# Reordering the start of a fused state-space and GeGLU kernel: x tile 2 loaded second, gate products before up products, tile 0 centred from a plain sum

## The chip, the cores and the metric

One core of a Trainium2 chip. The metric is the device time of one execution in microseconds (us), taken as the median of several executions. A profiled execution has a time of its own and a span inside it: the span runs from the first to the last instruction that the profiler shows.

## The reference, cut to what matters

The input x has 2048 rows of 512 numbers in bf16. Each row is normalised, and two branches are computed from the result and added to x:

```python
xn = layernorm(x)                                   # (x - mean) / sqrt(var + 1e-5), per row
# branch A: a diagonal complex recurrence over the 2048 rows, 512 states
h[t] = Lam_bar * h[t-1] + B_bar @ xn[t]
yA = 2 * Re(h @ C.T) + xn * Dskip
# branch B: a GeGLU feed-forward with 1376 hidden columns
yB = (gelu(xn @ w_gate) * (xn @ w_up)) @ w_down
out = x + yA + yB
```

## The kernel before, in words

**Blocks and tiles.** The 2048 rows are four blocks of 512, and a block is four tiles of 128 rows. In the regular path a block is normalised on the vector engine (`LN`, L637), transposed by DMA on SP's queue (`TR`, L708), multiplied by the gate and up weights (`GU`, L801) and by B (`BU`, L715), rotated and scanned on the vector engine (`CHAIN`, L734), and summed into the output (`DN`, L837).

**The start is special.** For block 0 the kernel does not wait for a complete layer norm. It subtracts the mean from a tile (`sub`, L920), transposes the centred tile on TensorE and copies it out of PSUM on ScalarE (`cent_T`, L652, copy at L669), and multiplies it, centred but not scaled, with the weights (`GT_mm`, L675). The factor 1/sqrt(var) is applied when the products leave PSUM (`GT_evac`, L691: gelu on ScalarE at L696, the product with the up half on VectorE at L699). It does this for the first 896 hidden columns in four ranges (`FR`, two of 192 columns and two of 256). `unit(j, r)` is one tile j times one range r, with gate and up in one matmul per 128 rows of the weights. For tiles 0 and 1 and the ranges 0 and 1 the gate products (`[0]`) and the up products (`[1]`) are separate matmuls of 192 columns, so that the gate can start before the up weights are there. Products of one tile and range share a PSUM bank.

**Filling.** TensorE runs seven matmuls on constants first (`fwarm`, L899) and further ones on constants between the first pieces of work (`fill`, L905; their results are not used).

**Means.** Tile 0's mean comes from `stats` on VectorE (L611: bn_stats then bn_aggr), tile 1's from a ScalarE copy with an accumulator (L926). `root` (L616) adds epsilon, takes the square root on GpSimd (L620), and `recip` (L624) inverts on VectorE; tiles 0 and 1 share one such chain, tiles 2 and 3 another.

**What sets the order.** TensorE and SP run their work in the order in which the program text creates it. VectorE, ScalarE and GpSimd run in the order of a planner (`Sched`), which simulates all engines with written-down durations and chooses by latest start times; `order_behind` (L129), which `ch` (L917) uses, pins one operation behind another. A wait on a semaphore is put in where data cross engines or come by DMA.

**Loads at the start.** SP's queue issues tile 0 of x, the first half of the first gate chunk (`WG0h[0]`: weight rows 0 to 255, columns 0 to 383), tile 2, the first up chunk, tile 3, and then the next chunks. The second gate chunk waits for `WG0h[0]` on SP (L502, `after=[gate0]`). Behind these in SP's queue come `tr_par`, block 0's four transposes, the load of block 1, the two transposed loads of B, Dskip, the load of block 2, and block 1's transposes. ScalarE's queue issues tile 1, `WG0h[1]` and three small parameter rows.

Of the kernel before, what the change touches and what calls it, by code (L numbers as in the profile page):

```python
# [9 lines left out]
ALU = mybir.AluOpType  # L10
# [67 lines left out]
class Sched:  # L78
# [95 lines left out]
    def _backward(self, span):  # L174
        ops = self.ops
        left = {op.id: len(op.users) for op in ops}
        late = {op.id: span for op in ops}
        ready = {e: [] for e in ENGINES}
        last = {e: [op for op in ops if op.eng == e] for e in INORDER}
        for op in ops:  # L180
            if left[op.id] == 0 and op.eng not in INORDER:
                ready[op.eng].append(op)
        busy = {e: span for e in ENGINES}
        begin = {}
        n = len(ops)
        while n:
            best = None
            for e in ENGINES:
                if e in INORDER:
                    if not last[e] or left[last[e][-1].id]:  # L190
                        continue
                    op = last[e][-1]
                else:
                    if not ready[e]:
                        continue
                    op = max(ready[e], key=lambda o: (min(busy[e], late[o.id]), o.finish, o.id))
                end = late[op.id] if op.kind == "dma" else min(busy[e], late[op.id])
                if best is None or end > best[0]:
                    best = (end, op)
            end, op = best  # L200
            e = op.eng
            if e in INORDER:
                last[e].pop()
            else:
                ready[e].remove(op)
            begin[op.id] = end - op.dur
            if op.kind == "dma":
                begin[op.id] = min(begin[op.id], busy[e] - op.issue)
                busy[e] = begin[op.id]
            else:  # L210
                busy[e] = begin[op.id]
            n -= 1
            for d in op.deps:
                late[d.id] = min(late[d.id], begin[op.id] - LAT(d, op))
                left[d.id] -= 1
                if left[d.id] == 0 and d.eng not in INORDER:
                    ready[d.eng].append(d)
        return begin

    def _forward(self, prio):  # L220
# [11 lines left out]
        nleft = len(ops)  # L232

        def rdy_time(op):
            return max([d.finish + LAT(d, op) for d in op.deps] + [op.nb])

        while nleft:
            best = None
# [52 lines left out]
    def emit(self):  # L291
        nc, es = self.nc, self.es
        order = self.order
        esem = {}
        for e in ENGINES:
            if any(op.kind == "eng" for op in order[e]):
                esem[e] = es.enter_context(nc.semaphore("q_" + e))
        cnt = {e: 0 for e in ENGINES}
        nd = 0
        for e in ENGINES:  # L300
            for op in order[e]:
                if op.kind == "eng":
                    cnt[e] += 1
                    op.sem, op.val = esem[e], cnt[e]
                else:
                    op.sem, op.val = es.enter_context(nc.semaphore("d%d" % nd)), 16
                    nd += 1
        self.n_sems = len(esem) + nd
        plan = {}
        nwait = 0  # L310
        for e in ENGINES:
            seen = {}
            prog = []
            for op in order[e]:
                need = {}
                for d in op.deps:
                    if d.kind == "eng" and d.eng == e and (e == "tensor" or d is op.behind):
                        continue
                    key = ("e", d.eng) if d.kind == "eng" else ("d", d.id)
                    if seen.get(key, 0) >= d.val:  # L320
                        continue
                    if key not in need or need[key].val < d.val:
                        need[key] = d
                for key, d in need.items():
                    seen[key] = d.val
                waits = [(d.sem, d.val) for d in need.values()]
# [12 lines left out]
        for (s, v) in final_waits:  # L339
            nc.sync.wait_ge(s, v)  # L340
# [10 lines left out]
def d_pe(n_list):  # L351
    return sum(n / 2.4 + 2.5 for n in n_list)
# [4 lines left out]
D_TINY = 160.0  # L357
# [4 lines left out]
def build(nc, ins, out):  # L362
    with ExitStack() as es:
# [110 lines left out]
        NM1 = A.alloc("NM1", [1], F32)  # L474

        def ld_x(b):
            return S.dma(lambda e, b=b: e.dma_start(
# [26 lines left out]

        def load_par():
            for q, nm in enumerate(("A_log_dt", "A_Lambda_re", "A_Lambda_im")):
                S.dma(lambda e, q=q, nm=nm: e.dma_start(PROW.ap[4 * q:4 * q + 4, :], ins[nm].rearrange("(s p) -> s p", p=128)),
                      1024, writes=[PROWq[q]], tag="ld_" + nm, queue="scalar", after=[half])
# [128 lines left out]
        def LN(b, js=range(4)):  # L637
# [3 lines left out]
            recip(qb, rq)  # L641
            norms(b, js, mn, rq, js[0])

        def SKIP(b):
# [5 lines left out]
        XCd = lambda j, k: XC_all.ap[:, k, 128 * j:128 * (j + 1)]  # L650

        def cent_T(j, banks, engs="A"):  # L652
            per = KD // len(engs)
# [21 lines left out]
        def GT_mm(j, r, bank, us, ks=range(KD)):  # L675
# [1 line left out]
            w = f1 - f0  # L677
            ci = max(0, r - 1)
            Wc = [(WGc, WUc)[u][ci] for u in us]
            if ci == 0 and us == [0] and len(ks) == 2:  # L680
                Wc = [WG0h[ks[0] // 2]]
            dst = PS[bank][:, w * us[0]:w * (us[-1] + 1)].rearrange("p (w f) -> p w f", w=len(us))

            def f(e):
# [1 line left out]
                for k in ks:  # L686
                    ins_ = e.matmul(dst, XCd(j, k), WGU[:, us[0]:us[-1] + 1, k, f0:f1], start=(k == 0), stop=(k == KD - 1))  # L687
                return ins_
            PE(f, d_pe([w * len(us)] * len(ks)), Wc + XCs[j][ks[0] // 2:ks[-1] // 2 + 1], [BANK[bank]], "GT")

        def GT_evac(j, r, bank, rs):  # L691
            f0, f1 = FR[r]
# [227 lines left out]
        def sub(j):  # L920
# [2 lines left out]
        load_par()  # L923
        load_W()
        tr_par()
        ACT(lambda e: e.activation(H0[3].ap[:, 0:D], X[1].ap, ACTF.Copy, scale=-1.0 / D, accum_out=NM1.ap), d_act(512) + 90,  # L926
            [X[1]], [H0[3], NM1], "mean1")
        ch(*stats(0, 0)); ch(sub(0))
        ch(V(lambda e: e.tensor_scalar(XN[1].ap, X[1].ap, NM1.ap, None, ALU.add), d_dve_ts4x(512), [X[1], NM1], [XN[1]], "sub"))
# [36 lines left out]
        unit(0, 2)  # L966
        unit(1, 2)
        unit(3, 0); unit(3, 1)
# [95 lines left out]
```

## Time and profile before

| | |
|---|---|
| median of 9 runs | 177.88 us (177.43 to 178.19) |
| profiled execution, its own time | 177.99 us |
| its span | 176.2 us |
| TensorE matmul busy | 172.8 us, 98% of the span |
| VectorE busy | 162.4 us, 92% |
| ScalarE busy | 90.3 us, 51% |
| GpSimd busy | 9.8 us, 6% |

Busy time is the time in which an engine has an instruction under way. Matmuls overlap: one of 128x512 is shown with 379 ns, while 49 of them in a row take 10.74 us, so 0.219 us each. For TensorE, the distance from one start to the next is therefore what counts. "Landing" of a DMA is the moment when its last part has signalled.

### The profile page before, as it was taken

The numbers are of one execution on the slowest core, as the hardware profiler recorded it, in microseconds if no ns is written. First come the engines' busy times: TensorE is split into PE (matmuls) and PEld (weight loads), VectorE is DVE, ScalarE is ACT, GpSimd is POOL, SyncE is SP. The second block draws the span as 40 slices with busy tenths as digits, with TensorE's granted clock in tenths as the row PEclk, the third lists the DMA queues.
The fourth block names the chain that finished last, engine by engine and source line by source line (L and its number), as shares of the span: only waits on it lengthen the run. The fifth ranks groups of instructions, "written<-read, shape, count | busy, mean of one in ns | idle before, by whom it ended". The sixth has DMA issues, their size and how long they took to land.

```text
span 176.2 us, 2489 instructions
## 1 busy us (share of the span) xinstructions
PE 172.8 (98%) x876; PEld 85.2 (48%) x891; DVE 162.4 (92%) x283; ACT 90.3 (51%) x169; POOL 9.8 (6%) x25
## 2 busy tenths in 40 slices
PE   8999999999999999999999999999999999999995
PEld 3954464444644444444644444444464444444454
DVE  6979999986999999979999999989999999999981
ACT  5466558899876899002676793000667790000000
POOL 3212030210000000011000000000000000000000
PEclk9999999999999999999999999999999999999999
DMA  5997995974999000012015000002101000000141
GB/s 159 333 298 173 203 237 110 115 149 97 194 299 214 4 0 0 2 39 80 4 33 113 5 0 0 4 0 76 43 0 30 4 0 0 0 0 0 33 149 61
DMA packets 33396, 14.36 MB, mean 81 GB/s; under 512 B 23688, under 2 KB 33384, under 8 KB 33384
## 3 DMA queue, kind: packets, MB, share of 16 engines
q1 hardware_dynamic: 32944, 13.87, 34.2%
q10 hardware_dynamic: 440, 0.33, 0.7%
q8 instruction: 7, 0.11, 0.3%
q14 instruction: 5, 0.04, 0.1%
HBM read 6.46 MB, written 2.10 MB: 49 GB/s over the span
## 4 chain that ended last, share of the span: by engine, by line
PE 98%; issue 0%; DVE 0%
PE PS L853 37%; PE PS L812 32%; PE PS L723 16%; PE PS L687 7%; PE PS L786 3%; PE PS L902 2%; PE PS L662 1%; PE PS L909 0%; DVE arena L871 0%
## 5 line engine op out<-in xcount | busy, mean ns | idle before, releaser
L853 PE MATMUL PS<-arena 128*128 128x512 bf16 (+3 forms) x317 | 65.9, 366 | 0.3
L812 PE MATMUL PS<-arena 128*128 128x512 bf16 x258 | 57.5, 379 | 0.3
L853 PEld LDWEIGHTS PS<-arena 128*128 128x128 bf16 (+1 forms) x323 | 30.8, 98 | 35.2
L812 PEld LDWEIGHTS PS<-arena 128*128 128x128 bf16 x264 | 25.8, 98 | 30.5
L756 DVE TENSOR_TENSOR_SCAN arena<-arena 128x512 bf16<-128x512 f32 x32 | 38.8, 1253 | 0.0
L827 ACT ACTIVATE arena<-PS 128x512 bf16<-128x512 f32 x33 | 19.7, 598 | 36.9 <-PE PS L812 33.3
L723 PE MATMUL PS<-arena 128*128 128x512 bf16 x125 | 27.8, 379 | 0.2
L831 ACT ACTIVATE arena<-PS 128x512 bf16<-128x512 f32 x33 | 19.7, 597 | 4.8 <-PE PS L812 4.6
L845 ACT ACTIVATE PS<-arena 128x512 f32<-128x512 bf16 (+2 forms) x17 | 9.6, 581 | 20.4 <-PE PS L853 19.7
L723 PEld LDWEIGHTS PS<-arena 128*128 128x128 bf16 x128 | 12.5, 98 | 14.8
L727 ACT ACTIVATE arena<-PS 128x512 bf16<-128x512 f32 x32 | 17.6, 595 | 2.3 <-PE PS L723 2.3
L871 DVE TENSOR_TENSOR arena<-PS,arena 128x512 bf16<-128x512 f32 (+2 forms) x17 | 10.8, 652 | 5.0 <-PE PS L853 4.5
L833 DVE TENSOR_TENSOR arena<-arena 128x512 bf16<-128x512 bf16 x33 | 13.0, 416 | 1.7 <-ACT arena L831 1.6
L687 PE MATMUL PS<-arena 128*128 128x192 bf16 (+2 forms) x80 | 13.4, 325 | 0.0
L613 DVE BATCH_NORM_STATS2 arena<-arena 128x6 f32<-128x512 bf16 x16 | 10.3, 682 | 0.7 <-DMA arena<-in_A_x_dram 0.7
L687 PEld LDWEIGHTS PS<-arena 128*128 128x128 bf16 x80 | 7.6, 102 | 4.8 <-issue 0.2
L743 DVE TENSOR_TENSOR arena<-arena 128x4096 bf16<-128x4096 bf16 (+1 forms) x5 | 9.2, 1858 | 0.5 <-ACT arena L608 0.5
L745 DVE TENSOR_TENSOR arena<-arena 128x4096 bf16<-128x4096 bf16 (+1 forms) x5 | 9.2, 1859 | 0.4 <-ACT arena L609 0.4
L696 ACT ACTIVATE arena<-PS,arena 128x192 bf16<-128x192 f32 (+1 forms) x16 | 6.7, 447 | 5.0 <-PE PS L687 4.0
L768 DVE TENSOR_TENSOR arena<-arena 128x4096 bf16<-128x4096 bf16 x4 | 9.2, 2289 | 0.1
L769 DVE TENSOR_TENSOR arena<-arena 128x4096 bf16<-128x4096 bf16 x4 | 9.1, 2285 | 0.0
L699 DVE SCALAR_TENSOR_TENSOR arena<-PS,arena 128x192 bf16<-128x192 f32 (+1 forms) x16 | 6.6, 444 | 1.2 <-ACT arena L696 1.0
(84 smaller groups left out, 110.4 us busy)
## 6 DMA issues: line engine op xcount, KB each, us to landing
out_dram<-arena SPq DMA_DIRECT2D x15, 128.0 KB, 1.7
arena<-in_A_x_dram SPq DMA_DIRECT2D x3, 512.0 KB, 4.9
arena<-in_B_w_down_dram SPq DMA_DIRECT2D x1, 1280.0 KB, 8.2
arena<-in_B_w_gate_dram SPq DMA_DIRECT2D x2, 256.0 KB, 4.2
arena<-in_B_w_up_dram SPq DMA_DIRECT2D x2, 256.0 KB, 4.6
arena<-in_B_w_gate_dram SPq DMA_DIRECT2D x1, 480.0 KB, 5.8
arena<-in_B_w_up_dram SPq DMA_DIRECT2D x1, 480.0 KB, 6.2
arena<-arena SPq DMA_TRANSPOSE x25, 2.5
```

Source lines behind the costliest of these rows:

```text
L613: return (V(lambda e: e.bn_stats(ST[tt].ap, X[tt].ap), d_dve_1x(512), [X[tt]], [ST[tt]], "bnst"), V(lambda e: e.bn_aggr(MVt[b][j].ap, ST[t ...
L687: ins_ = e.matmul(dst, XCd(j, k), WGU[:, us[0]:us[-1] + 1, k, f0:f1], start=(k == 0), stop=(k == KD - 1))
L723: ins_ = e.matmul(PS[bank][:, :], BBT[c][dk].ap[:, 128 * s:128 * (s + 1)], XNT[b].ap[:, dk, :], start=(dk == 0), stop=(dk == KD - 1))
L727: GATE["evBu"] = ACT(lambda e, bank=bank, k3=k3, s=s, c=c: e.activation(SSc[k3][s][c].ap, PS[bank][:, :], ACTF.Copy), d_act(512), [BANK[ba ...
L756: V(lambda e, g=g, rb=rb, init=init: e.tensor_tensor_scan(g.ap, rb, g.ap, init, ALU.mult, ALU.add), d_dve_scan(512), [g, PA[RRr]] + ([CARc ...
L812: ins_ = e.matmul(PS[bank][0:m, c0:c1], W.ap[:, dk, 128 * ft:128 * ft + m], XNT[b].ap[:, dk, c0:c1], start=(dk == 0), stop=(dk == KD - 1))
L827: GATE["last_gelu"] = ACT(lambda e, bg=bg, kk=kk, m=m: e.activation(GG[kk].ap[0:m, :], PS[bg][0:m, :], ACTF.Gelu_apprx_tanh), d_act(512), ...
L831: ACT(lambda e, bu=bu, kk=kk, m=m: e.activation(UPB[kk].ap[0:m, :], PS[bu][0:m, :], ACTF.Copy), d_act(512), [BANK[bu]], [UPB[kk]], "evU")
L833: V(lambda e, kk=kk, m=m, ft=ft, k2=k2: e.tensor_tensor(HTt[k2][ft].ap[0:m, :], GG[kk].ap[0:m, :], UPB[kk].ap[0:m, :], ALU.mult), d_dve_tt ...
L845: ACT(lambda e: e.activation(PS[bank][:, c0:c1], X[tt].ap[:, c0:c1], ACTF.Copy), d_act(c1 - c0), [X[tt]], [BANK[bank]], "seed")
L853: ins_ = e.matmul(PS[bank][:, c0:c1], l_[:, 128 * j:128 * (j + 1)], r_[:, c0:c1], start=False, stop=last and n == len(ops) - 1, skip_group ...
L871: V(lambda e: e.tensor_tensor(OUTB[ko].ap[:, c0:c1], PS[bank][:, c0:c1], XD[tt].ap[:, c0:c1], ALU.add), d_dve_1x(c1 - c0), [BANK[bank], XD ...
```

## The change

1. **Loads.** Tile 2 of x moves from third to second place on SP's queue, so `WG0h[0]` goes from second to third. ScalarE's queue keeps its order, now pinned.
2. **Tile 0's centring.** bn_stats, bn_aggr and one subtraction become a plain sum (`tensor_reduce`) and x*512 - sum in two parts, of 128 and 384 columns. `cent_T0` transposes each part by itself, and the ScalarE copy multiplies by 1/512.
3. **VectorE's order.** Behind that: tile 1's subtraction, tile 2's statistics and subtraction, and only then the statistics of tiles 0 and 1.
4. **TensorE's order.** Fillers go from five and four to one and two. Gate products of tile 0 for weight rows 0 to 127, tile 1's transposes, the rest of tile 0's gates, tile 2's transposes, gates of tiles 1 and 2, and then the up products of tiles 0, 1 and 2. Tile 2's ranges 0 and 1 are now split in gate and up as well.
5. **Block 3's layer norm.** `LN_act` takes the mean and the sum of squares with ScalarE accumulators in place of bn_stats and bn_aggr on VectorE. The subtraction and scaling stay on VectorE.
6. **The planner** treats an operation that is pinned behind a DMA on the same engine as free to start when the DMA has been issued, and no wait is put in.

```diff
-                late[d.id] = min(late[d.id], begin[op.id] - LAT(d, op))
+                late[d.id] = min(late[d.id], begin[op.id] + d.dur - d.issue if d is op.behind and d.kind == "dma" else begin[op.id] - LAT(d, op))
...
-                    if d.kind == "eng" and d.eng == e and (e == "tensor" or d is op.behind):
+                    if d.eng == e and (d is op.behind or d.kind == "eng" and e == "tensor"):
                         continue
...
         ld_x0(0)
-        S.order_behind(ld_x0(1, "scalar", [wrm]), GATE["table"])
+        x1 = S.order_behind(ld_x0(1, "scalar", [wrm]), GATE["table"])
+        ld_x0(2)
         gate0 = ld_wg0(0, "sync")
-        S.order_behind(ld_wg0(1, "scalar", [wrm]), GATE["table"])
-        ld_x0(2)
+        GATE["par"] = S.order_behind(ld_wg0(1, "scalar", [wrm]), x1)
...
+        def LN_act(b):
+            for j in range(4):
+                tt = 4 * b + j
+                xs = XN[tt % 8]
+                ACT(lambda e, j=j, tt=tt, xs=xs: e.activation(xs.ap, X[tt].ap, ACTF.Copy, scale=-1.0 / D, accum_out=NMBs[j].ap),
+                    d_act(512) + 190, [X[tt]], [xs, NMBs[j]], "mean")
+                ACT(lambda e, j=j, tt=tt, xs=xs: e.activation(xs.ap, X[tt].ap, ACTF.Square, bias=NMBs[j].ap, accum_out=SQBs[j].ap),
+                    d_act(512) + 190, [X[tt], NMBs[j]], [xs, SQBs[j]], "sq")
+            sbq, qb, rq = (cols(t, b, 0, 4) for t in (SBQ, QB, RQ))
+            V(lambda e: e.tensor_scalar(sbq.ap, SQB.ap, 1.0 / D, EPS_BF16, ALU.mult, ALU.add), D_TINY, [SQB], [sbq], "sbq")
...
+        def cent_T0(n, bank):
+            k0, k1 = ((0, 1), (1, KD))[n]
+            pt = PS[bank].bitcast(BF16)
...
+            PE(f, 56.0 * (k1 - k0), [XN0p[n], IDN], [BANK[bank]], "T0")
+            ACT(lambda e: e.activation(XC_all.ap[:, k0:k1, 0:128], pt[:, 0:128 * (k1 - k0)].rearrange("p (q t) -> p q t", t=128), ACTF.Copy, scale=1.0 / D),
+                d_act(128 * (k1 - k0)), [BANK[bank]], [XCs[0][n]], "evT")
...
-        ch(*stats(0, 0)); ch(sub(0))
+        ch(V(lambda e: e.tensor_reduce(SUM0.ap, X[0].ap, mybir.AxisListType.X, ALU.add), 630, [X[0]], [SUM0], "sum0"))
+        for n, (c0, c1) in enumerate(((0, 128), (128, D))):
+            ch(V(lambda e, c0=c0, c1=c1: e.tensor_scalar(XN[0].ap[:, c0:c1], X[0].ap[:, c0:c1], float(D), SUM0.ap, ALU.mult, ALU.subtract),
+                 100 + 0.5 * (c1 - c0), [X[0], SUM0], [XN0p[n]], "sub"))
         ch(V(lambda e: e.tensor_scalar(XN[1].ap, X[1].ap, NM1.ap, None, ALU.add), d_dve_ts4x(512), [X[1], NM1], [XN[1]], "sub"))
-        ch(*stats(0, 1))
+        ch(*stats(0, 2)); ch(sub(2))
+        ch(*stats(0, 0)); ch(*stats(0, 1))
         op, mn0, qb0, rq0 = root(0, 0, 2)
         ch(op)
-        ch(*stats(0, 2)); ch(sub(2))
+        ch(*stats(0, 3))
         ch(recip(qb0, rq0))
-
-        fill(5)
-        cent_T(0, tb, "AA")
-        cent_T(1, [wb])
-        ub = {(j, r): next_bank() for j in range(2) for r in range(2)}
-        for r in range(2):
-            GT_mm(0, r, ub[0, r], [0], (0, 1))
-        for r in range(2):
-            GT_mm(0, r, ub[0, r], [0], (2, 3))
-        fill(4)
-        for j in range(2):
-            ch(norms(0, [j], mn0, rq0, 0))
-        ch(*stats(0, 3)); ch(sub(3))
+        ch(sub(3))
         op, mn2, qb2, rq2 = root(0, 2, 4)
         ch(op)
         ch(recip(qb2, rq2))
+
+        ub = {(j, r): (3 + 2 * j + r) % 8 for j in range(3) for r in range(2)}
+        fill(1)
+        cent_T0(0, tb[0])
+        fill(2)
+        cent_T0(1, tb[1])
+        for r in range(2):
+            GT_mm(0, r, ub[0, r], [0], (0,))
+        cent_T(1, [wb])
+        for ks in ((1,), (2, 3)):
+            for r in range(2):
+                GT_mm(0, r, ub[0, r], [0], ks)
+        cent_T(2, tb, "AA")
+        norms(0, [0, 1], mn0, rq0, 0)
+        for r in range(2):
+            GT_mm(1, r, ub[1, r], [0])
+        for ks in ((0, 1), (2, 3)):
+            for r in range(2):
+                GT_mm(2, r, ub[2, r], [0], ks)
...
-        for r in range(2):
-            GT_mm(1, r, ub[1, r], [0])
-        for j in range(2):
+        for j in range(3):
             for r in range(2):
                 GT_mm(j, r, ub[j, r], [1])
                 GT_evac(j, r, ub[j, r], rss[j])
-                if j == 0 and r == 0:
-                    cent_T(2, tb)
-        unit(2, 0); unit(2, 1)
-        cent_T(3, [ub[0, 0]])
+        cent_T(3, [tb[0]])
+        rstate["n"] = tb[1]
         unit(0, 2)
...
-        LN(3); SKIP(3)
+        LN_act(3); SKIP(3)
```

More of the change, by code (lines that the diff above doesn't have):

```diff
@@ L234, in rdy_time @@
         def rdy_time(op):
-            return max([d.finish + LAT(d, op) for d in op.deps] + [op.nb])
+            return max([d.start + d.issue if d is op.behind and d.kind == "dma" else d.finish + LAT(d, op) for d in op.deps] + [op.nb])
         while nleft:
@@ L473, in build @@
         GATE["iotj"] = POOL(lambda e: e.iota(IOTJ.ap, [[1, 512]], base=0, channel_multiplier=0), 600, [], [IOTJ], "iotj")
-        NM1 = A.alloc("NM1", [1], F32)
+        NM1, SUM0 = A.alloc("NM1", [1], F32), A.alloc("SUM0", [1], F32)
         def ld_x(b):
@@ L506, in load_par @@
             for q, nm in enumerate(("A_log_dt", "A_Lambda_re", "A_Lambda_im")):
-                S.dma(lambda e, q=q, nm=nm: e.dma_start(PROW.ap[4 * q:4 * q + 4, :], ins[nm].rearrange("(s p) -> s p", p=128)),
-                      1024, writes=[PROWq[q]], tag="ld_" + nm, queue="scalar", after=[half])
+                GATE["par"] = S.order_behind(S.dma(lambda e, q=q, nm=nm: e.dma_start(PROW.ap[4 * q:4 * q + 4, :], ins[nm].rearrange("(s p) -> s p", p=128)),
+                      1024, writes=[PROWq[q]], tag="ld_" + nm, queue="scalar", after=[half]), GATE["par"])
         def tr_par():
@@ L642, in LN @@
             norms(b, js, mn, rq, js[0])
+        NMB, SQB = (A.alloc(n, [4], F32) for n in ("NMB", "SQB"))
+        NMBs, SQBs = ring(NMB, "NMB", 4), ring(SQB, "SQB", 4)
+        def LN_act(b):
[8 more added lines that the diff above has]
+            V(lambda e: e.tensor_scalar(sbq.ap, SQB.ap, 1.0 / D, EPS_BF16, ALU.mult, ALU.add), D_TINY, [SQB], [sbq], "sbq")
+            POOL(lambda e: e.tensor_tensor(qb.ap, sbq.ap, HALF.ap, ALU.pow), 1100, [sbq, HALF], [qb], "pow")
+            recip(qb, rq)
+            last = None
+            for j in range(4):
+                tt = 4 * b + j
+                last = S.order_behind(V(lambda e, j=j, tt=tt: e.tensor_scalar(
+                    XN[tt % 8].ap, X[tt].ap, NMBs[j].ap, rq.ap[:, j:j + 1], ALU.add, ALU.mult),
+                    d_dve_ts4x(512), [X[tt], NMBs[j], rq], [XN[tt % 8]], "ln_n"), last)
         def SKIP(b):
@@ L650, in build, with f @@
         XCd = lambda j, k: XC_all.ap[:, k, 128 * j:128 * (j + 1)]
+        XN0p = [Buf("XN0_%d" % n, "sb", XN[0].lo + 256 * n, XN[0].lo + (1024 if n else 256)) for n in range(2)]
+        def cent_T0(n, bank):
+            k0, k1 = ((0, 1), (1, KD))[n]
+            pt = PS[bank].bitcast(BF16)
+            def f(e):
+                ins_ = None
+                for k in range(k0, k1):
+                    ins_ = e.transpose(pt[:, 128 * (k - k0):128 * (k - k0 + 1)], XN[0].ap[:, 128 * k:128 * (k + 1)], IDN.ap)
+                return ins_
+            PE(f, 56.0 * (k1 - k0), [XN0p[n], IDN], [BANK[bank]], "T0")
+            ACT(lambda e: e.activation(XC_all.ap[:, k0:k1, 0:128], pt[:, 0:128 * (k1 - k0)].rearrange("p (q t) -> p q t", t=128), ACTF.Copy, scale=1.0 / D),
+                d_act(128 * (k1 - k0)), [BANK[bank]], [XCs[0][n]], "evT")
         def cent_T(j, banks, engs="A"):
@@ L679, in GT_mm @@
             Wc = [(WGc, WUc)[u][ci] for u in us]
-            if ci == 0 and us == [0] and len(ks) == 2:
+            if ci == 0 and us == [0] and len(ks) < KD:
                 Wc = [WG0h[ks[0] // 2]]
+            xc = XCs[0][ks[0] > 0:(ks[-1] > 0) + 1] if j == 0 else XCs[j][ks[0] // 2:ks[-1] // 2 + 1]
             dst = PS[bank][:, w * us[0]:w * (us[-1] + 1)].rearrange("p (w f) -> p w f", w=len(us))
@@ L688, in f @@
                 return ins_
-            PE(f, d_pe([w * len(us)] * len(ks)), Wc + XCs[j][ks[0] // 2:ks[-1] // 2 + 1], [BANK[bank]], "GT")
+            PE(f, d_pe([w * len(us)] * len(ks)), Wc + xc, [BANK[bank]], "GT")
         def GT_evac(j, r, bank, rs):
@@ L925, in build @@
         tr_par()
-        ACT(lambda e: e.activation(H0[3].ap[:, 0:D], X[1].ap, ACTF.Copy, scale=-1.0 / D, accum_out=NM1.ap), d_act(512) + 90,
-            [X[1]], [H0[3], NM1], "mean1")
-        ch(*stats(0, 0)); ch(sub(0))
+        S.order_behind(ACT(lambda e: e.activation(H0[3].ap[:, 0:D], X[1].ap, ACTF.Copy, scale=-1.0 / D, accum_out=NM1.ap), d_act(512) + 90,
+                           [X[1]], [H0[3], NM1], "mean1"), GATE["par"])
+        ch(V(lambda e: e.tensor_reduce(SUM0.ap, X[0].ap, mybir.AxisListType.X, ALU.add), 630, [X[0]], [SUM0], "sum0"))
+        for n, (c0, c1) in enumerate(((0, 128), (128, D))):
+            ch(V(lambda e, c0=c0, c1=c1: e.tensor_scalar(XN[0].ap[:, c0:c1], X[0].ap[:, c0:c1], float(D), SUM0.ap, ALU.mult, ALU.subtract),
+                 100 + 0.5 * (c1 - c0), [X[0], SUM0], [XN0p[n]], "sub"))
         ch(V(lambda e: e.tensor_scalar(XN[1].ap, X[1].ap, NM1.ap, None, ALU.add), d_dve_ts4x(512), [X[1], NM1], [XN[1]], "sub"))
-        ch(*stats(0, 1))
+        ch(*stats(0, 2)); ch(sub(2))
+        ch(*stats(0, 0)); ch(*stats(0, 1))
         op, mn0, qb0, rq0 = root(0, 0, 2)
         ch(op)
-        ch(*stats(0, 2)); ch(sub(2))
+        ch(*stats(0, 3))
         ch(recip(qb0, rq0))
-        fill(5)
-        cent_T(0, tb, "AA")
-        cent_T(1, [wb])
-        ub = {(j, r): next_bank() for j in range(2) for r in range(2)}
-        for r in range(2):
-            GT_mm(0, r, ub[0, r], [0], (0, 1))
-        for r in range(2):
-            GT_mm(0, r, ub[0, r], [0], (2, 3))
-        fill(4)
-        for j in range(2):
-            ch(norms(0, [j], mn0, rq0, 0))
-        ch(*stats(0, 3)); ch(sub(3))
+        ch(sub(3))
         op, mn2, qb2, rq2 = root(0, 2, 4)
```

## The prediction

> **What bounds the kernel now.** I read the chain that ended last first, by line and then in order of time.
>
> ```profile
> PE 98%; issue 0%; DVE 0%
> ```
> ```profile
> 0.78 3.15 PE PS L902 x7
> 3.92 0.53 PE PS L909 x5
> 4.46 0.85 PE PS L662 x8
> 5.31 1.28 PE PS L687 x8
> 6.59 0.23 PE PS L909 x4
> 6.82 0.99 PE PS L687 x12
> ```
>
> TensorE is the bound from 0.78 us to the last matmul at 174.4, without a pause beyond pieces of 0.05. Work taken off any other engine is worth nothing unless TensorE starts waiting for it. The only time to win on TensorE is in these lines: five fillers (0.53), four fillers (0.23), and between the starts of the transposes' last matmul and the first gate matmul 0.13 of real idleness (the trace has starts at 5.00 and 5.24, where 0.107 is one transpose).
>
> The same lines show two speeds. Five fillers took 0.53 us, 0.107 each, and four took 0.23, 0.058 each; eight gate matmuls of 192 columns took 1.28, 0.160 each, and twelve later ones 0.99, 0.082 each. The array runs at half speed until 6.4 us. Work moved ahead of 6.4 is worth half of what it takes there.
>
> Next, what releases the early work: VectorE's timeline, SP's timeline and the times to landing.
>
> ```profile
> 2.86 0.69 DVE L613 BATCH_NORM_STATS2 arena<-arena 128x6 f32<-128x512 bf16 x1 [0.53 <-DMA arena<-in_A_x_dram]
> 3.59 0.18 DVE L614 BATCH_NORM_AGGREGATE arena<-arena 128x2 bf16<-128x6 f32 x1
> 3.81 0.35 DVE L921 TENSOR_SCALAR arena<-arena 128x512 bf16<-128x512 bf16 x1
> 4.09 0.35 DVE L929 TENSOR_SCALAR arena<-arena 128x512 bf16<-128x512 bf16 x1
> ```
> ```profile
> 1.20 0.41 SPq L491 DMA_DIRECT2D arena<-in_B_w_gate_dram  x1
> 1.67 0.46 SPq L487 DMA_DIRECT2D arena<-in_A_x_dram  x1
> ...
> 4.13 0.38 SPq L483 DMA_DIRECT2D arena<-in_B_w_gate_dram  x1
> ```
> ```profile
> arena<-in_A_x_dram SPq DMA_DIRECT2D x3, 128.0 KB, 3.9
> ...
> arena<-in_B_w_gate_dram SPq DMA_DIRECT2D x1, 192.0 KB, 2.9
> arena<-in_B_w_gate_dram ACTq DMA_DIRECT2D x1, 192.0 KB, 4.0
> ```
>
> WG0h[0] is issued at 1.20 and lands at 4.12; SP waits for exactly that, its next issue being at 4.13. WG0h[1] is issued at 1.45 on ScalarE's queue and lands at 5.42. Tile 2 is issued at 1.67 and lands at 5.6.
>
> [...]the change of speed is at 6.4, 5.6 after the first matmul[...].[...] WG0h[1], issued 0.25 after WG0h[0], lands 1.3 later, close to tile 2.
>
> **The change part by part.**
>
> *Tile 0's centring.* Removed: 0.69 + 0.18 + 0.35 with their gaps, 2.86 to 4.16. Added: a sum of 512. [...]the nearest row, bn_stats, takes 0.69. I take 0.69; bounds 0.60 and 0.80. It ends at 3.56. [...]TensorE starts on it at about 3.93, against 4.25: 0.32 earlier, at half speed.
>
> *TensorE up to tile 2.* Warm-up ends at 3.72, one filler to 3.82, idle to 3.93, one transpose to 4.04, two fillers to 4.25, three transposes to 4.57. The first transpose's result is out at 3.93 + 0.31 = 4.24; ScalarE copies of 256 and 512 columns took 0.38 and 0.60, so 128 columns take 0.28: 4.28 to 4.56, and 0.14 on to TensorE as today (5.09 to 5.24): 4.70. From there two gate matmuls (0.32), four transposes (0.43), six gate matmuls (0.96): 1.71 at half speed, to 6.41. Tile 2's transposes and tile 1's gates then follow at once. Before, the same work ended at 6.42, but four fillers stood behind it until 6.66. Gain if the gate weights are there: 0.25.
>
> *The load order.* WG0h[0] is now asked for at 1.67, and WG0h[1] at 1.45 is ahead of it; tile 2 took that slot. Everything through tile 2 and both halves was 768 KB and complete at 5.6 before, its bulk by 4.9. A last-but-one place among these puts WG0h[0] at 4.6 (tile 2's third-slot first part landed at 4.59) to 5.6; I take 4.95. TensorE then starts the gates at 5.02 in place of 4.70. The 0.32 of waiting pushes work at half speed past 6.4, where it takes half: cost 0.16. WG0h[1] and the second copy (4.72 + 0.04 to 5.25) are not later than this.
>
> *Splitting tile 2's ranges.* Eight matmuls of 384 columns, 0.1625 each, become sixteen of 192 at 0.0825: +0.02.
>
> Sum: 0.25 - 0.16 - 0.02 = 0.07 gained on the profiled execution, 177.99 to 177.9. That execution stands 0.11 above the median; the same step from 177.88 gives 177.8.
>
> *VectorE's order and the up products.* Rows of 0.69 and 0.18 put tile 2 centred at 5.65 (needed at 6.4), the statistics of tiles 0 and 1 at 7.3, their reciprocal at 8.5 (7.01 before), tile 3 centred at 8.8 (needed at 9.9). The first up product ends near 8.3, so gelu waits about 0.3 for the reciprocal; TensorE does not, for its next reuse of a bank is at about 11.0 and drains of 0.33 to 0.4 each clear the early banks by then. Free; without that cover each late bank would cost its own delay.
>
> *SP behind WG0h[0].* The second gate chunk's issue moves from 4.13 to about 5.0. Queued behind that wait: five more weight loads, tr_par, block 0's transposes, block 1's load (issued 14.84), B's loads and block 1's transposes (last issued at 28.47, landed at 31.68, needed for block 1's B products at 32.0). The issues at 6.21 and 7.15 took 0.90 and 1.02 where others took 0.5[...]; block 1's statistics also sit behind a product that waits for TensorE at 19.9. I take 0 there, with 0.5 as the upper end.
>
> *Block 3's moments.* Four bn_stats (0.68) and four bn_aggr (0.18) leave VectorE, 3.4 us; eight ScalarE passes of 0.63 + 0.19 (the L926 row) come in, 6.6 us. The cover is this:
>
> ```profile
> 81.96 0.60 ACT L827 ACTIVATE arena<-PS 128x512 bf16<-128x512 f32 x1 [11.62 <-PE PS L812]
> ```
>
> ScalarE is idle from 70.3 to 82.0, and the results are needed at 91 (transposes) and 99.4 (first product of block 3). [...]at worst two table loads of 1.28, and 6.6 + 2.6 still fits in 11.6. Zero. If the planner places the passes among busy copies before 70, one pass of 0.82 ahead of a needed copy may cost up to 0.8.
>
> **The rivals.**
>
> *The gates are there in time* (by 4.7): the full 0.25, and up to 0.57 if all nine fillers and the gap count (0.67 at half speed plus 0.23). Time 177.5. For it: tile 2 is the smaller transfer. Against: WG0h[0] took 2.9 from issue to landing in the second slot, and third-slot tile 2 took 3.9; 1.67 + 2.9 would be 4.6 only without the other half's traffic.
>
> [...]
>
> *A later wait in mid-kernel:* block 1's transposes late at 32.0, or a re-planned ScalarE that holds a bank: +0.5, 178.4. It decides once the SP shift exceeds the slack of 0.3 at 32.0.
>
> *The change does nothing visible* is the forecast's own neighbourhood.
>
> **How the numbers follow.** About 0.2%, 0.36 us, is what a measurement of this kernel can tell from no change. Forecast (177.8, own range 177.5 to 178.2): 0.50, of it 0.45 same, 0.02 faster, 0.03 slower. Gates in time: 0.14, of it 0.10 faster. Slow array: 0.12, slower. Later wait: 0.24, of it 0.20 slower. Faster 0.12, same 0.53, slower 0.35. The low end 177.4 leaves out 0.04, the high end 178.8 the slow array and 0.03 more.
>
> **What would show it.** First transpose at 3.9; a TensorE wait on DMA between 4.57 and 5.0; transposes and gates at 0.107 and 0.160 each in a row from there to 6.4; tile 2's transposes straight behind; SP's second gate chunk at 5.0; ScalarE's Square passes between 70 and 82; no pause at 32.0 or 99.4. A change of speed after 8 us without gaps to explain it would be the slow array. A landing of WG0h[0] before 4.7 or after 5.5, or any TensorE wait after 10 us, would make the prediction wrong.

## The result, and the profile after

The changed kernel takes 179.02 us (median of 10 executions, 178.19 to 179.69) against 177.75 us for the kernel before beside it (32 executions, 177.43 to 178.38). The ratio is 1.007, with a 95% interval of 1.0055 to 1.0084: slower by about 1.24 us. The forecast of 177.8 was wrong, and so was its range of 177.4 to 178.8. Ratios in this document leave out executions over 1.5% above the fastest of their kernel, while medians and ranges count all of them.

The profiled execution took 179.17 us, 1.18 more than that of before (177.99). First the chain that ended last, by engine:

```profile
PE 93%; DMA 2%; DVE 1%; issue 1%; SPq 0%; ACT 0%; ACTq 0%; DVEq 0%
```

TensorE had 98% of this chain. Now a DMA and VectorE are on it. In order of time (start, length, what), its early part is:

```profile
1.66 4.21 DMA arena<-in_B_w_gate_dram
5.91 0.34 PE PS L725 x2
6.25 0.22 PE PS L699 x4
6.47 0.50 PE PS L725 x6
...
19.32 0.50 DVE arena L737
19.82 0.18 issue
20.00 5.12 PE PS L850 x23
```

The gate weights that were asked for at 1.66 set the start of TensorE's work, at 5.91 and not at 5.02 as forecast. The regular products of block 0 (L850, L812 in the old numbering) start at 20.00, against 18.83 in the same view of the kernel before:

```profile
18.83 5.13 PE PS L812 x23
```

That is 1.17 later, and the execution is 1.18 longer: everything is lost by 20 us, and nothing after. The same view shows what the array did: six gate matmuls took 0.50, 0.083 each, so it ran at full speed by 6.5. The trace's clock records put the change of speed at 3.95 in this execution, where it was 6.37 in the one before.

TensorE's waits (total, times, longest) name the two places:

```profile
PE PS L725 <- DMA arena<-in_B_w_gate_dram: 1.5, 1, 1.5
PE PS L850 <- DVE arena L737: 0.9, 1, 0.9
```

SP's timeline (start, length, queue, what) shows what stood behind the same load:

```profile
1.66 0.43 SPq L491 DMA_DIRECT2D arena<-in_B_w_gate_dram  x1
...
5.88 0.37 SPq L483 DMA_DIRECT2D arena<-in_B_w_gate_dram  x1
...
11.73 5.18 SPq L749 DMA_TRANSPOSE arena<-arena  x4
```

The second gate chunk left at 5.88 in place of 4.13, and block 0's transposes began to be issued at 11.73. In the kernel before they began at 9.61:

```profile
9.61 5.19 SPq L711 DMA_TRANSPOSE arena<-arena  x4
```

The releaser in the second wait, a product of VectorE, is not what held TensorE. The semaphore that TensorE's own wait names is that of block 0's fourth transposed tile. Of its 16 parts, 15 had signalled by 18.12 and the last at 19.65, and TensorE went on at 20.00, 0.35 later. In the execution before, the last part came at 16.03, when nobody was waiting. A later run (block 3 undone, below) has the same VectorE product at 19.13, after its TensorE had started L850 at 18.94.

The parts that were meant to bring something did what they say. VectorE's timeline (L966 is the plain sum, L968 the two parts, L959 the subtraction for tile 2):

```profile
2.84 0.69 DVE L966 TENSOR_REDUCE arena<-arena 128x1 f32<-128x512 bf16 x1 [0.54 <-DMA arena<-in_A_x_dram]
3.56 0.48 DVE L968 TENSOR_SCALAR arena<-arena 128x128 bf16<-128x128 bf16 x2
...
5.27 0.35 DVE L959 TENSOR_SCALAR arena<-arena 128x512 bf16<-128x512 bf16 x1
```

The sum took 0.69, tile 0's first transpose started at 3.88 (4.25 before), and tile 2 was centred at 5.62. Block 3's moments sit where ScalarE was idle, from 74.1 to 79.5, and no pause of TensorE follows 20 us:

```profile
74.09 0.63 ACT L651 ACTIVATE arena<-arena 128x512 bf16<-128x512 bf16 x1 [2.78 <-issue]
...
79.28 0.19 ACT L653 ACTIVATION_READ_ACCUMULATOR arena<-arena 128x1 f32 x1
```

### The profile page after: what moved, and what is told of

It reads as the page before. It is cut to its first block, busy times and chain, and to the rows that moved or that the text cites. A ratio compares the mean times of both kernels' runs of the same rounds, so it can differ in the third digit from the quotient of the medians.

```text
span 177.4 us, 2515 instructions
## 1 busy us (share of the span) xinstructions
PE 171.7 (97%) x878; PEld 84.3 (48%) x893; DVE 159.0 (90%) x277; ACT 96.1 (54%) x186; POOL 9.8 (6%) x24
## 4 chain that ended last, share of the span: by engine, by line
PE 93%; DMA 2%; DVE 1%; issue 1%; SPq 0%; ACT 0%; ACTq 0%; DVEq 0%
PE PS L891 37%; PE PS L850 32%; PE PS L761 15%; PE PS L725 6%; PE PS L824 3%; DMA arena<-in_B_w_gate_dram 2%; DVE arena L737 1%; SPq L487 0%; PE PS L699 0%; ACT arena L734 0%; DVE arena L600 0%; DVE arena L909 0%; DVE arena L559 0%; ACTq L337 0%; DVEq L337 0%
## 5 line engine op out<-in xcount | busy, mean ns | idle before, releaser
L850 PE MATMUL PS<-arena 128*128 128x512 bf16 x258 | 57.5, 379 | 1.2 <-DVE arena L737 0.9
L850 PEld LDWEIGHTS PS<-arena 128*128 128x128 bf16 x264 | 25.7, 98 | 31.4 <-issue 1.2
L725 PE MATMUL PS<-arena 128*128 128x192 bf16 (+2 forms) x88 | 12.8, 302 | 1.5 <-DMA arena<-in_B_w_gate_dram 1.5
L613 DVE BATCH_NORM_STATS2 arena<-arena 128x6 f32<-128x512 bf16 x12 | 7.8, 679 | 1.0 <-DMA arena<-in_A_x_dram 1.0
```

The costliest lines, as they stand in the source:

```text
L850: ins_ = e.matmul(PS[bank][0:m, c0:c1], W.ap[:, dk, 128 * ft:128 * ft + m], XNT[b].ap[:, dk, c0:c1], start=(dk == 0), stop=(dk == KD - 1))
```

## The experiments

The expectations name four theories. Q and V were open once the two traces had been compared; H and D came after the first four runs.

- **Q, the queue:** the loss is the pause at 19 to 20 us. SP waits for the late `WG0h[0]`, and what stands behind it in SP's queue comes late. As recorded, the way from SP to the pause led over the parameter transpose, GpSimd and VectorE; the semaphore named above puts block 0's fourth transposed tile in their place.
- **V, VectorE's order:** the new order on VectorE makes the pause by itself, whatever SP does.
- **H, half speed:** the idle time in front of the first gate matmuls keeps the array at half speed for longer in a share of the executions, and these move the median.
- **D, plain delay:** an idle stretch costs its own length and no more.

All times, each beside its own runs of the kernel before (whose medians were 177.60 to 177.88). Where a kernel's executions fall in two groups, the ratio understates the upper one, and the median says more.

| kernel | median (range), executions | ratio to before, 95% |
|---|---|---|
| changed kernel | 179.02 (178.19 to 179.69), 10 | 1.0070 [1.0055, 1.0084] |
| 1. SP's wait removed | 179.46 (177.73 to 180.48), 11 | 1.0066 [1.0037, 1.0094] |
| 1. again | 179.34 (177.94 to 180.32), 8 | 1.0078 [1.0041, 1.0115] |
| 2. gate half second again | 178.19 (177.71 to 180.18), 22 | 1.0029 [1.0015, 1.0043] |
| 3. load order alone, on before | 179.20 (178.28 to 179.94), 6 | 1.0076 [1.0054, 1.0098] |
| 4. block 3 undone | 179.03 (177.76 to 180.44), 19 | 1.0054 [1.0030, 1.0078] |
| 5. 1 with fillers in the wait | 178.60 (178.16 to 178.76), 5 | 1.0051 [1.0039, 1.0063] |
| 6. changed, with fillers | 178.51 (178.01 to 178.89), 6 | 1.0049 [1.0036, 1.0063] |
| 7. centring alone | 177.83 (177.81 to 178.15), 21 | 1.0014 [1.0008, 1.0021] |
| 8. tile 2 on ScalarE's queue | 178.79 (177.71 to 180.99), 12 | 1.0067 [1.0036, 1.0098] |
| 9. 8 with fillers | 178.06 (177.64 to 180.63), 14 | 1.0018 [1.0008, 1.0029] |
| 10. idle stretch alone, on before | 179.22 (178.86 to 180.73), 6 | 1.0108 [1.0075, 1.0141] |
| 11. 10 with fillers | 179.03 (178.79 to 179.64), 6 | 1.0080 [1.0067, 1.0093] |

### 1. SP does not wait for the gate half

```diff
-            ld_w(WG, WGc, ins["B_w_gate"], ci, after=[gate0] if ci == 1 else ())
+            ld_w(WG, WGc, ins["B_w_gate"], ci)
```

> The kernel after, with one wait taken away: SP no longer waits for the first half of the first gate chunk before it issues the second gate chunk. Order of work on every engine unchanged. Theory Q (the queue): the pause of 1.1 us on TensorE at 18.9 to 20.0 comes from SP, which stood still until 5.88 and so brought the parameter transpose, GpSimd's power and VectorE's L556 late, ahead of the drains. Then here the second chunk goes out at 3.2, the transpose lands about 13.5, the pause at 18.9 is gone, the wait for the gate half (4.3 to 5.9) stays: 177.9 to 178.2. Theory V (VectorE's new order by itself makes the drains late): pause stays, 179.0.

The median did not fall: 179.46. Theory Q alone cannot be the cause. In the profiled execution (178.39 us) the pause at 19 is gone and L850 starts at 19.24, but not because the transposes got ahead: two of SP's issues, at 4.78 and 6.34, took 1.52 and 1.23 where others took 0.5, and the fourth transposed tile landed at 18.58. What differed from the changed kernel is that no part of it came 1.5 us behind the others, as its last part had done there.

The executions fell in two groups, so the same kernel was run again.

> The same kernel as e1_no_gate_wait, a second profile beside the next one on the same chip. Theory H[...]: times from 177.7 to 180.5 again, median 178.5 to 179.6, and a profile from a slow execution shows transposes at 0.107 and gate matmuls at 0.160 until 7 us or later. Theory D (the spread comes from when the weights land): every profile has the fast array by 7, and the landing of the gate half differs by 1 us and more.

179.34, and two groups again: of 19 executions in both runs, 9 lie between 177.73 and 178.81 and 10 between 179.46 and 180.48. One profile was taken in each group. The chain in order of time, lower group (178.39 us):

```profile
6.37 0.22 PE PS L699 x4
6.59 0.49 PE PS L725 x6
...
19.24 2.97 PE PS L850 x13
```

and upper group (180.05 us):

```profile
6.55 0.43 PE PS L699 x4
6.98 0.96 PE PS L725 x6
...
20.82 1.24 PE PS L850 x5
```

Up to tile 1's transposes (L699, at 6.37 and 6.55) the two executions are within 0.18 us of each other. From there the same instructions take twice as long: 0.96 for six gate matmuls against 0.49. The clock records have the array at full speed from 3.70 in the first and only from 9.62 in the second. The first regular product starts 1.58 later, and the execution is 1.66 longer. That is the difference that theory H describes, seen in one execution of each group; experiments 5 and 6 test whether the idle time is its cause.

### 2. The gate half second again

```diff
-        ld_x0(2)
         gate0 = ld_wg0(0, "sync")
+        ld_x0(2)
```

> The kernel after, with the loads in the old order: first gate half second on SP, tile 2 of x third. Order of work on every other engine unchanged. Theory Q: the gate half lands at 4.1, the 1.5 us wait for it is gone, SP goes on at 4.1 and the pause at 18.9 is gone. Tile 2 lands at 5.6 instead of 3.5, so VectorE has it centred at about 6.95 and TensorE may wait up to 0.6 for its transposes: 177.5 to 178.2. Theory V: VectorE's chain is even later than in the kernel after, the pause at 18.9 stays: 178.5 to 179.2.

178.19, a ratio of 1.0029: more than half of the loss goes with this one line. What stays is a wait for tile 2, which in the third place landed at 5.54 and was centred at 6.87:

```profile
PE PS L699 <- DVE arena L959: 0.9, 1, 0.9
```

The order in which TensorE now works needs tile 2 early and the gate half early. Each took the other's place.

### 3. The load order alone, on the kernel before

```diff
+        ld_x0(2)
         gate0 = ld_wg0(0, "sync")
         S.order_behind(ld_wg0(1, "scalar", [wrm]), GATE["table"])
-        ld_x0(2)
```

> The kernel before, with only the loads swapped: tile 2 of x second, first gate half third. Order of work on every other engine unchanged. Theory Q: the gate half lands at 5.9, TensorE waits for it about 0.7 us longer (less where the array is still slow), SP stands still until 5.9, and the pause before the first 128x512 gate and up work appears as in the kernel after: 178.4 to 179.1. Theory V: only the early wait, no pause there: 177.9 to 178.3.

179.20, a ratio of 1.0076: the exchange of two loads by itself costs as much as the whole change. VectorE has its old order here, so theory V isn't needed for the loss. The profile (179.15 us) shows three waits on TensorE:

```profile
PE PS L812 <- ACT arena L696: 0.8, 1, 0.8
PE PS L687 <- DMA arena<-in_B_w_gate_dram: 0.7, 1, 0.7
PE PS L723 <- DMA arena<-arena: 0.4, 1, 0.4
```

In order of time, 0.7 is for the gate half (it landed at 5.63), 0.8 stands in front of the regular products, and 0.4 ends at 33.2 with block 1's transposes. The releaser named for the second is again not what held TensorE: its own wait names the fourth transposed tile, whose last part came at 19.10 (the other 15 by 17.55), and TensorE went on 0.35 later, as in the changed kernel. In this execution the array was fast from 4.05, before the first of these waits, so a slow array has no part in them.

### 4. Block 3's layer norm undone

```diff
-        LN_act(3); SKIP(3)
+        LN(3); SKIP(3)
```

> The kernel after, with block 3's layer norm back on VectorE. Both theories: no difference from the kernel after, 179.0 (178.8 to 179.3), with the two waits where they were. If ScalarE's passes for block 3 cost something: below 178.7.

179.03, as the changed kernel: these runs show no cost and no gain of this part. The executions spread as widely as in experiment 1, nine of 19 up to 178.67 and nine from 179.26 to 180.44. The profile of one of the quick ones (178.11 us) also settles the releaser. VectorE's timeline, then TensorE's:

```profile
19.13 0.48 DVE L737 SCALAR_TENSOR_TENSOR arena<-PS,arena 128x256 bf16<-128x256 f32 x1 [0.16 <-issue]
```
```profile
18.94 2.32 PE L850 MATMUL PS<-arena 128*128 128x512 bf16 x10
```

L850 starts 0.19 before the product that was named as its releaser starts. The fourth transposed tile had landed at 17.03, although SP waited for `WG0h[0]` here too, and TensorE did not pause.

### 5 and 6. Fillers in the wait

```diff
         cent_T0(1, tb[1])
+        fill(12)
         for r in range(2):
             GT_mm(0, r, ub[0, r], [0], (0,))
```

Once on the kernel of experiment 1, and once on the changed kernel with SP's wait kept.

> e1_no_gate_wait with twelve more fillers on TensorE ahead of the gate matmuls, where it waited for the gate half: 1.28 us at half speed or 0.70 at full, inside the wait. Theory H: [...]it turns fast no later than in the kernel before, the spread narrows to about 1 us and the median falls to 178.0 to 178.4. Theory D: fillers do nothing or cost a little, spread and median as in e1_again.

> The kernel after with the same twelve fillers; SP's wait for the gate half stays. Theory Q (with it, the end of the start phase is set by SP, the parameter transpose, GpSimd and VectorE's L556 ahead of the drains, whatever the array does): 178.6 to 179.1, the pause before the first 128x512 gate and up work stays or grows. If theory H alone explains the loss of the kernel after: 178.0 to 178.4.

With constants multiplied in the idle stretch the medians are lower. Without SP's wait the median went from 179.34 to 178.60 on the same chip, and the spread from 2.4 us to 0.6. With SP's wait it is 178.51, against 179.02 for the changed kernel, which ran beside other runs of the kernel before. The intervals of the ratios overlap in both pairs; what is clear is the upper group, which has four of eight executions without fillers on that chip (179.96 and more) and none of the 11 with them (178.89 at most). TensorE's timeline of the first:

```profile
4.53 1.49 PE L947 MATMUL PS<-const-bfloat16-1.0 128*128 128x128 bf16 x12
6.05 0.35 PE L725 MATMUL PS<-arena 128*128 128x192 bf16 x2
```

The first gate matmuls start no earlier than in the two profiles without fillers, 6.05 against 6.03 and 6.05, but they run at full speed: 0.35 for two, against 0.50 in the upper group. The sixth kernel's profile shows them beside a slow array. It was slow when they came (the twelve took 1.28, 0.107 each), they ran on past the landing at 5.58, and the gates started at 5.79. But the view of TensorE's waits has none after its start at 0.77, and the array was fast from 6.56. In the profile of experiment 1's upper group TensorE waited for 1.4 us, up to 6.05, and the array stayed slow until 9.62.

Both medians came out 0.1 to 0.2 above what H expected. Each beside its own kernel before, fillers give back 0.74 of 1.72 us without SP's wait and 0.38 of 1.27 with it; 0.9 to 1.0 stays. SP's wait makes no difference between the two (178.60 and 178.51), and the sixth kernel's profile has no pause at 19 (fourth tile at 18.39, L850 at 19.36), which theory Q had wanted.

### 7. The centring alone

Loads, VectorE's order, tile 2's place and block 3 as before; only the sum in two parts, the gates of tile 0 in three steps, the fewer fillers, ScalarE's pinned queue and the planner's new rule are those of the change. Against the changed kernel:

```diff
-        ld_x0(2)
         gate0 = ld_wg0(0, "sync")
+        ld_x0(2)
...
-        ch(*stats(0, 2)); ch(sub(2))
         ch(*stats(0, 0)); ch(*stats(0, 1))
...
-        cent_T(2, tb, "AA")
-        norms(0, [0, 1], mn0, rq0, 0)
...
-        LN_act(3); SKIP(3)
+        LN(3); SKIP(3)
```

> The old load order, VectorE's old order behind tile 0, tile 2's transposes and ranges where they were, block 3 on VectorE; of the change only tile 0's plain sum in two parts, its gate matmuls in four steps, one and two fillers in place of five and four, and the pinned queue of ScalarE. By the prediction's step (0.25 gained where the weights are there): 177.5 to 177.7. If the centring is worth nothing: 177.8 to 178.0.

177.83, a ratio of 1.0014: slightly slower, where a gain of 0.25 had been priced. The chain in order of time:

```profile
6.87 0.19 DVE arena L614
...
7.09 0.36 DVE arena L959
...
7.50 0.40 PE PS L699 x4
```

TensorE is ahead, its last gate matmul starting at 7.16, and then stands until VectorE has centred tile 2. Up to 7.50 VectorE is the bound, and the quicker start is handed back there. The times fit: eight of the 21 executions took 177.81 and none less, while the kernel before beside them goes down to 177.27. The two profiles alone do not show the loss (L850 starts at 18.67, against 18.83), but the array was fast from about 5.1 in this one and from 6.37 in that of before.

### 8 and 9. Tile 2 on ScalarE's queue

This was meant to give both loads an early place, and so to beat both kernels.

```diff
-        ld_x0(2)
         gate0 = ld_wg0(0, "sync")
-        GATE["par"] = S.order_behind(ld_wg0(1, "scalar", [wrm]), x1)
+        x2_ = S.order_behind(ld_x0(2, "scalar", [wrm]), x1)
+        GATE["par"] = S.order_behind(ld_wg0(1, "scalar", [wrm]), x2_)
```

> The changed kernel with one difference: tile 2 of x is loaded on ScalarE's queue between tile 1 and the second half of the first gate weights, so that the first half stands second on SyncE again; every order of work on the engines is that of the change. If the loss is the late first half (5.6 to 6.0 us) with its two consequences, TensorE finds the half at about 4.1 to 4.6 and tile 2 at 4.1 to 5.0, waits less than 0.4 us in front of the first gate matmuls, and the median is 177.4 to 177.8, at or slightly under the kernel before. If the second half now lands after 5.9, the wait only changes its place and the median is about 178 to 178.6. If the loss lies in the order of the work rather than in the loads, 178.8 to 179.3.

In the profiled execution (177.71 us) `WG0h[0]` and tile 2 were there in time, the wait was 0.4, for the second half (landed at 6.30), and L850 started at 18.80. But six of twelve executions took 179.5 to 180.99, so the median lies just under the range expected if the order of work were the cause. None of the six was profiled. Four of them have a mean granted clock of 0.99, where all of experiment 1 have 1.00 (the record of its slow execution begins only with full speed), so it isn't shown that the same slow array is behind both. This stretch was filled as well, by `fill(6)` in front of the matmuls that need the second half.

> The kernel with tile 2 on ScalarE's queue, with 6 filler matmuls in the stretch of about 0.4 us in which TensorE waited for the second half of the first gate weights. Its executions without fillers fell in two groups of six, 177.71 to 178.09 and 179.5 to 180.99. Theory H: the upper group goes, all executions lie in 177.6 to 178.4 and the median is 177.8 to 178.1. If the groups have another cause than the idle stretch, some executions stay above 179.4 and the median is between 178 and 179.5.

178.06, and one execution of 14 above 179.4 in place of six of 12. H had wanted all at 178.4 or below; 178.75 and 180.63 lie above it. The two experiments ran on different chips. In the profile (177.81 us) the array was fast when the fillers came (the gate matmuls before them took 0.33 for two, against 0.48 in experiment 8), and 0.5 us of waiting stayed behind them. By its ratio it is the quickest kernel with the change's order of work, and still 0.18% behind the kernel before.

### 10 and 11. An idle stretch by itself

To separate the idle stretch from everything else of the change, the kernel before, with its loads as they were, waits in front of its first gate matmuls for the first chunk of up weights too. (The planned orders on VectorE and ScalarE moved with it in places.)

```diff
-            PE(f, d_pe([w * len(us)] * len(ks)), Wc + XCs[j][ks[0] // 2:ks[-1] // 2 + 1], [BANK[bank]], "GT")
+            PE(f, d_pe([w * len(us)] * len(ks)), Wc + (WUc[0:1] if j == 0 and us == [0] and ks == (0, 1) else []) + XCs[j][ks[0] // 2:ks[-1] // 2 + 1], [BANK[bank]], "GT")
```

and, in the second, `fill(14)` behind tile 1's transposes.

> The kernel before, with its loads in their old order; only the first two gate matmuls also wait for the first chunk of up weights, which lands at about 6.7 us, so that TensorE idles about 1.6 us from 5.1 to 6.7. (The planned orders on VectorE and ScalarE move with it in places.) Theory H[...]: a spread of more than 2 us between executions and a median of 179.5 to 180. Theory D, that an idle stretch costs its own length and no more: 178.7 to 179.2, with a spread of about 1.1.

> The kernel before with the same added wait for the first up chunk, and 14 filler matmuls in the idle stretch ahead of it, on the same orders of VectorE and ScalarE. Theory H: the array is fast when the chunk lands, the median is 178.6 to 179.0 and the spread at most 1.2, lower than without fillers by 0.7 or more. Theory D: the same time as without the fillers, 178.7 to 179.2, within 0.2.

179.22 and 179.03: as medians these fit D better than H. Four of six executions without fillers (178.86 to 179.35) lie where those with fillers lie (178.79 to 179.64). The other two took 180.58 and 180.73. One of them was profiled, and its chain shows the slow array:

```profile
7.12 1.44 PE PS L687 x8
8.56 0.43 PE PS L909 x4
```

The same eight gate matmuls and four fillers in the filled kernel's profile:

```profile
6.95 0.82 PE PS L687 x8
7.77 0.23 PE PS L909 x4
```

Full speed came at 10.13 in the first and at 3.88 in the second, where the 14 fillers took 0.82 (0.059 each) and 1.1 us of waiting stayed. So a late start of 1.7 to 1.9 us (the gates at 6.95 and 7.12, in place of 5.23) costs about 1.4 us in the median with fillers in the wait (179.03 less 177.60), and in some executions without them 1.6 to 1.7 us more; the one of these with a profile shows the slow array. They were two of six here and ten of 19 in experiment 1; none of six with fillers does not settle it here, and with so few the share is open.

## Why the prediction was wrong

**Wrong: where the gate half lands.** The step that failed is "a last-but-one place among these puts WG0h[0] at 4.6 to 5.6; I take 4.95", and with it "cost 0.16". It landed at 5.87 in the changed kernel and at 5.58 to 6.01 in the other profiles with this load order: at or past the upper end. Half of its 16 parts had signalled by 5.19. I had priced the place by the bulk of the traffic before it, but TensorE went on at 5.91, behind the last part. It waited 1.46, not 0.32. (The prediction's own sign of being wrong, a landing after 5.5, came true.) Experiments 2 and 3 show that this exchange carries the loss: undone, it takes the ratio from 1.0070 to 1.0029, and alone it gives 1.0076. Of the medians' loss, 0.9 to 1.0 us stays where fillers take the upper group away (experiments 5 and 6), so that part is not the slow array of the next point.

**Wrong in its chance: the slow array.** It had 0.12, and a change of speed after 8 us for its sign. Such changes came, at 9.62 in experiment 1 and at 10.13 in experiment 10, in one profile each, behind waits of 1.4 and 1.8. The upper group has ten of the 19 executions of experiment 1, and none of the 11 of experiments 5 and 6. The chance was weighed for a wait of 0.45, from 4.57 to 5.02. In the changed kernel the wait was 1.46. How long a wait it takes is not shown. For the changed kernel itself the share is not shown: its ten executions run from 178.19 to 179.69 without a gap. The pause at 19 may fill it in; experiment 4's kernel, the same but for block 3 and without a pause in its profile, spreads from 177.76 to 180.44.

**Wrong place: SP behind the gate half.** I took 0, and 0.5 as the upper end, at 32.0. The shift at SP was 1.75, not 0.87, and where it met a pause was 19 to 20, for 0.93 in the profiled execution; only experiment 3 paused for block 1's transposes, 0.4 at 33.2. I had not looked at the slack of block 0's own transposes, which was 2.8 (landed at 16.03, wanted at 18.83). The shift alone does not use it up: in experiments 4 and 6, with the same wait, the fourth tile landed at 17.03 and 18.39 and nothing paused. In the two profiles with a pause, one late part came besides. Taking the wait off brought no gain in the medians (179.46 and 179.34 against 179.02; 178.60 against 178.51).

**Right as a size, wrong as a gain: the centring.** The sum at 0.69 (0.69 forecast), the two parts at 0.25 and 0.32, the first transpose at 3.88 (3.93 forecast): the times held. But "gain if the gate weights are there: 0.25" fell with experiment 7, which is 0.2 slower in the median. With the weights early and tile 2 in its old place, VectorE's way to tile 2 was the bound until 7.50. With tile 2's early place and the weights late, DMA was. With the weights second and tile 2's work early (experiment 2), tile 2's load and its statistics were, at 6.92. The saving of 0.3 sat in front of three other ends, each of which took over in one of the runs.

**Right:** block 3's moments at zero (experiment 4), with the cover named; no table load came with Square, as the changed kernel has the same three table loads of 1.28 as before. Also right: the late reciprocal stopped nobody on TensorE.

The sum for the profiled execution, in the terms of the prediction: L850 starts 1.17 later. Of that 0.93 is the pause at 19 to 20, and 0.24 what is left of the wait of 1.46 after the earlier centring, the fillers taken out and an array that was fast 2.4 us earlier than in the profile before. In experiment 1's execution of the upper group, 1.6 comes from the array instead. The two need not add: there the fourth tile landed at 20.04, before the slow array needed it at 20.82.

## What to carry to other kernels

Price a load that is moved behind others by the last part of the last transfer in its new company, not by where the bulk of the bytes goes by; here that was the difference between 4.95 and 5.87. Count an idle stretch of TensorE at the start twice: here it cost most of its length (1.4 of 1.7 in experiment 11), and in some executions 1.6 to 1.7 us more from an array that stayed slow. Filler matmuls in the wait took the second cost away in experiments 5 and 6, so taking fillers out is not free when loads shift. Before a shorter first step is called a gain, the other chains that feed the next steps should be listed with their ends; here the weights, tile 2's load and VectorE's statistics took over in turn.

## What was not expected of the hardware

**When the array turned fast.** TensorE begins at 0.77 or 0.78. The clock records of nine profiles have the moment at which full speed began: 3.70 (experiment 1, lower group), 3.88 (11), 3.95 (the changed kernel), 4.05 (3), 6.17 (8), 6.37 (the kernel before), 6.56 (6), 9.62 (1, upper group) and 10.13 (10). The five profiles without such records show the change in the spacing of the matmuls, at about 4.4 (experiment 9), 5.1 (7) and 5.3 (2), and somewhere in 4.4 to 5.7 (4) and in 5.7 to 6.1 (5). So two executions of one kernel lie 5.92 apart (experiment 1). In the four with 4.05 or less the array was fast before the waits of 0.7 to 1.5 began, and fast behind them: 0.083 for a gate matmul in the changed kernel, after 1.46. In the two with the latest moments it was slow when a wait of 1.4 and of 1.8 began, and slow behind it: 0.160 for a gate matmul in experiment 1's upper group. With fillers in the wait (experiment 6) it was slow too, and fast from 6.56. What sets the moment is not shown.

**One part of sixteen, 1.5 us late.** The last of the 16 parts of block 0's fourth transposed tile came 1.53 us after the fifteenth in the changed kernel (18.12, 19.65), and 1.55 in experiment 3 (17.55, 19.10). In experiments 2, 5, 7 and 8 the third tile had the same, by 1.54 to 1.55 us (14.93 and 16.47 in experiment 7), where nobody was waiting for it. All other parts of these two tiles came within 0.3 in all profiles. What holds one part back is open: no run was made for it.
